# A fused RWKV5 attention and squared-ReLU FFN: a fixed issue order, W1 cast on chip, and PSUM banks allocated in pairs

## The chip, the cores and the metric

The kernel runs on one core of one Trainium2 chip. The metric is the device time of one execution in microseconds (us). Times of one kernel mostly agree within 1 to 1.5%. Every kernel below was timed against the kernel before, on the same chip, in alternating rounds. The rounds of different experiments ran at other times and on other chips, so two experiments are best compared by their ratios to the kernel before. Each profile is one execution; its span is about 2 us shorter than the device time. On a single core a run is called slow when it lies over 1.5% above the fastest run of the same kernel; comparisons use fast runs.

Engine names in the profile: PE is TensorE (matmul), PEld its weight load, DVE is VectorE, ACT is ScalarE, POOL is GpSimd, SP is SyncE, which here issues most DMAs. A `q` after the name is the engine's sequencer or its DMA queue. The granted clock (`PEclk`) is the share of its full clock that the throttle granted to TensorE. The matmuls of these kernels write to tiles in PSUM, which the code uses as eight banks of 128x512 fp32.

## The reference

```
B, H, S, D = 4, 8, 768, 48
for t in range(S):                                   # linear attention with decay
    cur = einsum('bhd,bhe->bhde', u * k[t], v[t])
    y[t] = einsum('bhd,bhde->bhe', r[t], state + cur)
    state = w * state + einsum('bhd,bhe->bhde', k[t], v[t])
x = y as rows of 384                                 # 3072 tokens x 384
h = maximum(x @ w_in, 0)                             # 384 -> 2048
out = (h * h) @ w_out                                # 2048 -> 384
```

Inputs and outputs are fp32. The kernel cuts the 3072 tokens into 24 units of 128 tokens (one batch element, one chunk of 128 steps each). The state is passed from chunk to chunk, so units 0 to 3 are the first chunk of the four batch elements, 4 to 7 the second, and so on.

## The kernel before

Each unit goes through these steps. The short names are those of the code.

- Loads of r, k and v (192 KB each, in rows of 192 bytes, since one head has 48 fp32 values).
- `kh`, `rh`: k and r times powers of the decay w. `P0`, `P1`, `du`, `dv`: the diagonal term with u. `vb`: v as bf16.
- `T`, `rkT`: transposes on PE and their copy by ACT (later units use a transposing DMA).
- `A` (8 matmuls with 48 rows, into two PSUM banks), `Bm` (DVE masks A), `Y`, `xs`, and `U`, `ts`, `S` for the state.
- `X`, `xT`: x transposed for the FFN.
- FFN for a group of two units: `F1` (x times a slice of W1, 6 matmuls of 128x256 into one PSUM bank), `re` (ReLU on ACT), `sq` (square, on ACT or on DVE; DVE multiplies the bank by the ReLU), `F2` (4 matmuls of 128x384 for a quarter of W2), then `os` and `out`.

All weights, 2 x 1.5 MB as bf16, stay in SBUF. They come by the software DMA queue of POOL, which converts fp32 to bf16 on the way. The steps are given to a small list scheduler in Python that orders them by priorities and estimated durations, and also chooses the buffer of each tile.

```python
POOLS = dict(..., bank=3, bankH=3, bankO=2, Bm=3, xs=3, xT=2, hr=6, hq=28, ...)
...
    banks = [psum.tile([128, 512], FP32, name=f"bank_{j}") for j in range(8)]
    first = {"bank": 0, "bankH": POOLS["bank"], "bankO": POOLS["bank"] + POOLS["bankH"]}

    def bank(var, pool):
        return banks[first[pool] + slot[var]]
...
    s_wb = st("wb", "SP", 0.1, dma=0.6, prio=-200, emit=lambda: nc.sync.dma_start(out=wb..., in_=flat_rows(w)))
...
            Ws.append(st(f"W{part}{s}", "POOL", 0.78, [s_g], ...))     # W1, W2: nc.gpsimd.dma_start, after a gate
...
    def f_Bm(i, e):
        def go():
            nc.vector.tensor_mul(Bmb[slot[f"Bm{i}"]][:, e], heads(f"bA{i}{e}", "bank", 128), mask_b)
...
    def f_relu(g, s):
        def go():
            hp = bank(f"bH{g},{s}", "bankH").rearrange("p (a b) -> p a b", a=2)
            nc.scalar.activation(hrb[slot[f"hr{g},{s}"]], hp, AF.Relu)
...
    def f_sq(g, s, eng):
        def go():
            hr, hq = hrb[slot[f"hr{g},{s}"]], hqb[slot[f"hq{g},{s}"]]
            if eng == "ACT":
                nc.scalar.activation(hq, hr, AF.Square)
            else:
                hp = bank(f"bH{g},{s}", "bankH").rearrange("p (a b) -> p a b", a=2)
                nc.vector.tensor_mul(hq, hp, hr)
```

No step names a semaphore. The framework sees which tiles an instruction reads and writes, and puts in the waits itself.

## Time and profile before

| | before |
|---|---|
| time, median of 3 runs (range) | 184.03 us (182.91 to 185.37) |
| span of the profile | 180.6 us |
| PE busy | 160.6 us, 89% |
| granted TensorE clock | 1.00 |
| PE busy from 60 to 160 us | 99.55 of 100 us |
| PE busy from 0 to 60 us | 44.00 of 60 us |

The profile's page of the kernel before. The first lines give each engine's busy time and its number of instructions. The next give busy tenths of each engine in 40 equal slices of the span. After that come the shares of the chain of work that ended last, and two groups of instructions with busy time, mean duration in ns, and the idle time just before them.

```profile
span 180.6 us, 4082 instructions
...
PE 160.6 (89%) x1592; PEld 118.2 (65%) x1592; DVE 128.6 (71%) x216; ACT 117.5 (65%) x214; POOL 106.8 (59%) x116
...
PE   0344769899999999999999999999999999999991
...
DVE  3399998997388838959979696778777889631310
...
DMA  3999999999949649979799799897896255221102
...
PE 79%; DVE 9%; DMA 4%; ACT 2%; SPq 2%; issue 1%; DVEq 0%
...
L604 PE MATMUL bank<-xT,W 128*128 128x256 bf16 x576 | 73.8, 273 | 0.4 <-DVE hq L629 0.3
L638 PE MATMUL bank<-W,hq 128*128 128x384 bf16 x384 | 72.0, 326 | 0.0
```

There are two regimes. After the ramp PE is busy nine tenths or more in every slice up to the end, and the FFN matmuls (L604 is F1, L638 is F2) have almost no idle time before them. In the ramp both DVE and the DMA engines are busy. The table of stretches of the kernel before says the same with numbers (start and end, length, busy us and number of instructions of each engine, granted clock, share of the DMA engines, GB/s):

```profile
core 0: us, PE busy (x) PEld busy (x) DVE busy (x) ACT busy (x) POOL busy (x), PEclk, DMA share, GB/s
10.00:15.00 5.00, 2.49 (x23) 1.60 (x23) 4.97 (x9) 1.93 (x4) 1.89 (x3) 1.00 1.06 198
...
30.00:40.00 10.00, 8.93 (x97) 7.22 (x96) 9.49 (x19) 9.82 (x19) 2.13 (x3) 1.00 1.27 185
60.00:160.00 100.00, 99.55 (x1027) 73.59 (x1026) 77.85 (x126) 69.02 (x129) 76.31 (x75) 1.00 0.78 160
```

From 10 to 15 us DVE is busy 4.97 of 5 us, and the DMA engines are full too while they move only 198 GB/s.

A piece of the chain of work of the kernel before, from its middle (start, us, what):

```profile
130.13 1.97 PE bank L604 x18
132.10 0.33 PE bank L454 x8
132.43 0.76 PE bank L604 x6
133.19 0.65 PE bank L638 x4
```

Six F1 matmuls take 0.66 us, four F2 matmuls 0.65. `A` (L454) takes 0.33 us, and the six matmuls after it 0.76, so 0.1 us more. PE does not leave the chain in this piece. The timeline of the same place (start, us, engine, line, operation, count, idle time before it and what ended it) shows why:

```profile
129.97 2.13 PE L604 MATMUL bank<-xT,W 128*128 128x256 bf16 x18
...
130.82 1.25 ACT L618 ACTIVATE hr<-bank 128x512 bf16<-128x512 f32 x2 [2.02 <-PE bank L604]
...
131.45 0.69 DVE L629 TENSOR_TENSOR hq<-bank,hr 128x512 bf16<-128x512 f32 x1 [0.28 <-ACT hr L618]
```

The 18 matmuls are three slices of F1, in three banks. ACT begins the ReLU of the first slice at 130.82 while PE goes on with the next until 132.10; DVE squares from 131.45 in the same time.

### The profile page before, as it was taken

To read this page: it belongs to the slowest core of one execution; us is meant where nothing else is said; L and a number is where in the kernel's file an instruction comes from. 1 tells how busy PE (TensorE), PEld (TensorE's weight loads), DVE (VectorE), ACT (ScalarE), POOL (GpSimd) and SP (SyncE) were. 2 spreads that over 40 slices of the span, in tenths; PEclk is the share of its full clock that TensorE was granted. 3 is DMA by queue.
4 is the path that set the end of the run, shared out by engine and by line. 5 is a ranking of instruction groups with operands and counts; after the bars stand their busy time and mean duration, and the time that the engine had idled before them with its cause. 6 is when DMAs were issued, how large, how long until landed. Compare 5 with 4: busy or idle time off the path is not lost.

```text
span 180.6 us, 4082 instructions
## 1 busy us (share of the span) xinstructions
PE 160.6 (89%) x1592; PEld 118.2 (65%) x1592; DVE 128.6 (71%) x216; ACT 117.5 (65%) x214; POOL 106.8 (59%) x116
## 2 busy tenths in 40 slices
PE   0344769899999999999999999999999999999991
PEld 0222557778766867758678677677686776777760
DVE  3399998997388838959979696778777889631310
ACT  2641528986793886827776758579298495496851
POOL 2346998024940999599879977986968980000000
PEclk9999999999999999999999999999999999999999
DMA  3999999999949649979799799897896255221102
GB/s 85 207 195 216 196 191 193 184 185 222 225 116 241 149 82 253 184 152 241 142 216 204 122 237 202 138 225 164 167 228 155 71 120 80 65 65 47 41 2 87
DMA packets 105794, 28.44 MB, mean 157 GB/s; under 512 B 98864, under 2 KB 105776, under 8 KB 105776
## 3 DMA queue, kind: packets, MB, share of 16 engines
q1 hardware_dynamic: 102064, 25.04, 68.1%
q0 software_dynamic: 3712, 3.15, 11.0%
q8 instruction: 12, 0.20, 0.5%
q14 instruction: 6, 0.05, 0.1%
HBM read 20.84 MB, written 4.72 MB: 142 GB/s over the span
## 4 chain that ended last, share of the span: by engine, by line
PE 79%; DVE 9%; DMA 4%; ACT 2%; SPq 2%; issue 1%; DVEq 0%
PE bank L638 34%; PE bank L604 32%; PE bank L454 4%; PE bank L483 3%; DMA ub<-in_u_dram 2%; DMA xT<-xs 2%; PE bank L478 2%; PE bank L429 2%; DVE rk L382 2%; SPq L351 2%; DVE xs L506 2%; DVE dv L411 2%; PE bank L495 2%; DVE Bm L467 1%; ACT rkT L436 1%
## 5 line engine op out<-in xcount | busy, mean ns | idle before, releaser
L618 ACT ACTIVATE hr<-bank 128x512 bf16<-128x512 f32 x96 | 55.9, 595 | 29.4 <-PE bank L604 27.6
L604 PE MATMUL bank<-xT,W 128*128 128x256 bf16 x576 | 73.8, 273 | 0.4 <-DVE hq L629 0.3
L638 PE MATMUL bank<-W,hq 128*128 128x384 bf16 x384 | 72.0, 326 | 0.0
L604 PEld LDWEIGHTS <-W 128*128 128x128 bf16 x576 | 55.0, 98 | 11.8 <-issue 0.9
L638 PEld LDWEIGHTS <-hq 128*128 128x128 bf16 x384 | 36.1, 98 | 19.3
L629 DVE TENSOR_TENSOR hq<-bank,hr 128x512 bf16<-128x512 f32 x48 | 32.6, 683 | 17.4 <-ACT hr L618 17.4
L467 DVE TENSOR_TENSOR Bm<-bank,maskJT 128x512 bf16<-128x512 f32 x48 | 31.1, 681 | 8.2 <-PE bank L454 8.1
L388 POOL TENSOR_TENSOR P<-ldr,ldk 128x384 f32<-128x384 f32 x24 | 28.2, 1177 | 9.9 <-DMA ldr<-in_r_dram 9.9
L528 POOL TENSOR_TENSOR S0W<-ts,WLm 128x384 bf16<-128x384 f32 x16 | 16.5, 1031 | 29.1 <-DVE ts L522 28.9
L626 ACT ACTIVATE hq<-hr 128x512 bf16<-128x512 bf16 x48 | 30.2, 630 | 1.1
L397 POOL TENSOR_TENSOR P<-P,ub 128x384 f32<-128x384 f32 x22 | 22.9, 1043 | 1.4
L411 DVE TENSOR_TENSOR dv<-ldv,du 128x384 f32<-128x384 f32 x24 | 21.2, 883 | 0.5
L506 DVE TENSOR_TENSOR xs<-bank,dv 128x384 bf16<-128x384 f32 x24 | 13.3, 555 | 11.1 <-PE bank L483 10.7
L651 ACT COPY os<-bank 128x384 f32<-128x384 f32 x24 | 11.4, 476 | 12.4 <-PE bank L638 12.1
L429 PE MATMUL bank<-identity,rk 128*128 128x128 bf16 x64 | 7.5, 273 | 10.5 <-DVE rk L382 10.2
L382 POOL TENSOR_TENSOR rk<-ldr,Wt 128x384 bf16<-128x384 f32 x16 | 16.6, 1040 | 0.1
L382 POOL TENSOR_TENSOR rk<-ldk,Wkhat 128x384 bf16<-128x384 f32 x16 | 16.0, 1002 | 0.0
L429 PEld LDWEIGHTS <-rk 128*128 128x128 bf16 x64 | 5.5, 120 | 12.4 <-DVE rk L382 11.5
L417 ACT CAST vb<-ldv 128x384 bf16<-128x384 f32 x24 | 11.6, 507 | 2.9 <-DMA ldv<-in_v_dram 2.9
L403 DVE TENSOR_REDUCE du<-P 128x8 f32<-128x384 f32 x24 | 13.0, 543 | 0.2 <-POOL P L397 0.2
L454 PE MATMUL bank<-rkT 48*128 48x128 bf16 x192 | 10.6, 233 | 2.5 <-ACT rkT L436 2.2
L483 PE MATMUL bank<-vb,Bm 128*128 128x48 bf16 x192 | 12.2, 189 | 0.4 <-DVE Bm L467 0.4
(40 smaller groups left out, 101.7 us busy)
## 6 DMA issues: line engine op xcount, KB each, us to landing
out_dram<-os SPq DMA_DIRECT2D x24, 192.0 KB, 2.6
ldk<-in_k_dram SPq DMA_DIRECT2D x11, 384.0 KB, 4.1
ldr<-in_r_dram SPq DMA_DIRECT2D x11, 384.0 KB, 5.0
ldv<-in_v_dram SPq DMA_DIRECT2D x11, 384.0 KB, 4.0
W<-in_moe_w_in_dram POOLq DMA_DIRECT2D x4, 384.0 KB, 8.9
W<-in_moe_w_out_dram POOLq DMA_DIRECT2D x4, 384.0 KB, 15.6
ldk<-in_k_dram SPq DMA_DIRECT2D x2, 192.0 KB, 4.2
ldr<-in_r_dram SPq DMA_DIRECT2D x2, 192.0 KB, 4.5
```

What stands on the lines that cost most here:

```text
L382: e.tensor_mul(rk[slot[f"rk{i}"]][:, j, :, 0:D], ld[x][slot[f"{x}P{i // 2}"]][:, i % 2], tab)
L388: nc.gpsimd.tensor_mul(P0b[slot[f"P0{i}"]], ld["r"][slot[f"rP{i // 2}"]][:, i % 2], ld["k"][slot[f"kP{i // 2}"]][:, i % 2])
L397: (nc.vector if eng == "DVE" else nc.gpsimd).tensor_mul(t, t, ub)
L411: nc.vector.tensor_mul(dvb[slot[f"dv{i}"]], ld["v"][slot[f"vP{i // 2}"]][:, i % 2], du_b)
L454: nc.tensor.matmul(heads(f"bA{i}{e}", "bank", 128)[:, hc, :], rkT[p0 : p0 + D, HP + hc, :], rkT[p0 : p0 + D, hc, :], start=True, stop=True ...
L467: nc.vector.tensor_mul(Bmb[slot[f"Bm{i}"]][:, e], heads(f"bA{i}{e}", "bank", 128), mask_b)
L483: nc.tensor.matmul(Y[:, hc, D * e : D * (e + 1)], Bm[:, e, hc, :], vb[:, 2 * hc + e, :], start=(c == 0), stop=True, skip_group_check=True,)
L604: nc.tensor.matmul(hp[:, fi, :], W1[s // 2][:, c, 128 * f : 128 * (f + 1)], xt[:, c, :], start=(c == 0), stop=(c == CCH - 1), skip_group_c ...
L618: nc.scalar.activation(hrb[slot[f"hr{g},{s}"]], hp, AF.Relu)
L626: nc.scalar.activation(hq, hr, AF.Square)
L629: nc.vector.tensor_mul(hq, hp, hr)
L638: nc.tensor.matmul(o, hqb[slot[f"hq{g},{f // 2}"]][:, f % 2, L * j : L * (j + 1)], W2[q][:, f % 4, :], start=(f == 0), stop=(f == FCH - 1) ...
```

## The change

The intent: begin the FFN earlier and shorten the ramp.

- The scheduler is removed. One long string fixes the order of all steps and the buffer of each tile.
- w and u are no longer broadcast by DMA. Four rows are loaded, and a DVE shuffle spreads them over the partitions.
- W1 comes as fp32 over the SP queue between the first loads, and ACT, DVE and POOL cast it. W2 stays on the software queue.
- The first two FFN groups have one unit (128 tokens) each.
- `A` of two units is issued back to back from unit 8 on.
- `Bm` is one DVE operation of 128x1024. For that, two banks must be one tile.
- Loads are single units, with five buffers each for r, k and v.

The diff, cut to its core (the order string alone has some 80 lines):

```diff
-def order_steps(steps, pools, sw_rate=0.75, hw_rate=0.17):
-    ...
-POOLS = dict(ldr=2, ldk=2, ldv=2, ..., bank=3, bankH=3, bankO=2, ..., xT=2, ...)
+GROUPS = [1, 1, 2, 2, 2, 2, 2, 2, 2, 2, 2, 2, 2]
+POOLS = dict(ldr=5, ldk=5, ldv=5, ws=4, ..., bank=4, bankH=2, bankO=2, ..., xT1=2, xT2=2, ...)
+ORDER = """
+w:A ld.k.3:S/0 u:S tab:A ld.k.1:S/1 ld.k.0:S/2 ld.r.0:S/0 ld.r.1:S/1 shw:D wc:S logw:A shu:D ld.r.2:S/2 Wk:A
+ld.k.2:S/3 Wt:A kh.3:G/0 ld.v.0:S/0 lW.0.2:S/0 ld.v.1:S/1 kh.1:D/1 kh.0:D/2 lW.0.0:S/1 rh.0:D lW.0.1:S/2 ...
+... T.1:P/2 dv.0:G Tc.1:D/1 Y.0:P/3 U.0:P/0 ld.r.11:S/4 cW.0.2:A S0.0:D rh.2:G xs.0:D/0
+ld.k.9:S/4 ...
-    banks = [psum.tile([128, 512], FP32, name=f"bank_{j}") for j in range(8)]
-    def bank(var, pool):
-        return banks[first[pool] + slot[var]]
+    pairs = [psum.tile([128, 2, 512], FP32, name=f"banks_{j}") for j in range(4)]
+    def bank(var, kind="b"):
+        j = first[kind] + slot[var]
+        return pairs[j // 2][:, j % 2]
-            nc.vector.tensor_mul(Bmb[slot[f"Bm{i}"]][:, e], heads(f"bA{i}{e}", "bank", 128), mask_b)
+        def Bm(e, i):
+            a = pairs[slot[f"bA{i}"] // 2].rearrange("p a (b c) -> p (a b) c", c=128)
+            e.tensor_mul(Bmb[slot[f"Bm{i}"]], a, mask_b)
+        def shw(e):
+            e.stream_shuffle(wb.rearrange("p a b -> p (a b)"), wrow, [0] * 32)
+        def AA(e, i):
+            Do.A(e, i)
+            Do.A(e, i + 1)
+        def cW(e, a, s):
+            copy(e, W1[s]..., wsb[...])          # fp32 staged in SBUF -> bf16
```

## The prediction

> **What bounds it now.** The table of stretches shows two regimes. From 40 us to the last matmul (177.1 us) TensorE is busy throughout at clock 1.00; the waits of PE list almost nothing there, and PE has 79% of the chain of waits. Six 128x256 FFN matmuls take 0.655 us, four 128x384 ones 0.65, so the FFN needs 96 x 0.655 + 96 x 0.65 = 125 us. With attention (A 0.33 + 0.1 after it, Y about 0.37, U 0.17, some transposes) I sum 153 us of PE work. The other 24 us are lost in the ramp: PE is busy 10.2 of the first 25 us, and the first FFN matmul starts at 27.5 us, when the first W1 slice lands (issued from 18.2 us). DVE is busy 4.6 to 5.0 of every 5 us between 10 and 25 us: the ramp is bound by DVE and loads (DMA share over 1.0).
>
> **What the change does.**
> 1. Broadcast loads of w and u (192 KB each, 3.6 and 4.1 us from issue to landing; u held DVE up 1.7 us) become four rows and two DVE shuffles (estimate 0.5 us each, as 384-wide DVE operations take 0.55). The queue is freed of some 2 us; the tables come 0.5 us earlier.
> 2. W1 comes over the hardware queue as fp32, between the first loads, cast by ACT, DVE and POOL. From 2 us per 384 KB load of 192 B packets I estimate 2 to 2.5 us per 786 KB slice of 2 KB packets, 1.6 us per cast; first slice at 14 us, first FFN matmul at 16. W2 stays on the software queue, its first slice earlier.
> 3. FFN groups of one unit let the FFN begin after unit 0. Their 96 matmuls are 128 wide; the transposes show 56 ns for that: 0.2 us of PE more.
> 4. In the ramp DVE work goes to POOL; Bm becomes one 128x1024 operation (two took 1.28 us; little saved).
> 5. A of two units back to back saves about 0.1 us of mode change for each of 8 pairs: 0.8 us.
> 6. FFN banks fall from 3 to 2. A bank is held 0.65 + 0.2 + 0.6 + 0.7 = 2.2 us when DVE squares, against 3.1 us between uses: little slack, so I allow 1 us of stalls.
>
> **On the critical path.** Before, PE runs without gaps from about 34.6 us, with 4.6 us of FFN done and units 0 to 3 nearly through. After, I expect this at 31 us (DVE work up to unit 3 sums to 25 us), with 8 us of FFN done. Gain 3.6 + 3.4 = 7 us, plus 0.8 for A, minus 1; the tail is unchanged.
>
> **Prediction: 176.5 us, range 171.5 to 181.5.** Faster by over 2%: 0.83; within 2%: 0.13; slower: 0.04.
>
> **What shows it.** First FFN matmul at 15 to 18 us; first F2 before 25; PE full from 29 to 32 us; waits of PE between 40 and 160 us below 2 us; one slow matmul after a pair of A, not two; PE busy sum about the same.
>
> **What would make it wrong.** Fixed order without slack: one late load (two for units 9 and 11 sit early in the queue, and W2 shares the DMA engines) stalls PE in order. Two FFN banks, or POOL and DVE holding each other up (dv took 883 ns on average instead of 555; the Trainium skill, "SBUF — State Buffer", "Who interferes with whom", describes an exclusively locked port pair), would show as PE waits in mid-kernel. If the ramp works better than I think, the gain is 10 us.

## The result, and the profile after

| | before | after |
|---|---|---|
| time, median (range) in these rounds | 184.70 us (182.91 to 185.76) | 216.94 us (214.73 to 221.09) |
| span of the profile | 180.6 us | 215.7 us |
| PE busy | 160.6 us | 167.1 us |
| PE busy, 60 to 160 us | 99.55 us | 86.46 us |
| PE busy, 0 to 60 us | 44.00 us | 37.58 us |

The ratio is 1.174, with a 95% interval of 1.165 to 1.184: slower by 17%. A ratio is the mean time of one kernel's fast runs over that of the other's fast runs of the same rounds, so it is not quite the ratio of the medians that are quoted. One of the four runs after counted as slow and is left out of the ratio. The outputs are correct.

The page of the kernel after (same parts as before):

```profile
span 215.7 us, 4244 instructions
...
PE 167.1 (78%) x1640; PEld 121.7 (56%) x1640; DVE 122.3 (57%) x196; ACT 115.5 (54%) x205; POOL 115.8 (54%) x129
...
PE   0267488479978888988988889896978788787882
...
DMA  3999999998849977788967788683252240311002
...
PE 50%; ACT 18%; DVE 16%; DMA 8%; issue 3%; SPq 3%; POOL 1%; DVEq 0%; POOLq 0%
```

PE is no longer full after the ramp: it stands at seven to nine tenths to the end. Its share of the chain fell from 79% to 50%, and ACT and DVE stepped in with 34%, though both are busy for a smaller share of the span than before. An engine that is in the chain and idle nearly half of its time is waiting in turn with the others. The table of stretches of the kernel after confirms that the loss goes on all along:

```profile
60.00:160.00 100.00, 86.46 (x881) 63.35 (x881) 66.57 (x101) 58.44 (x108) 70.70 (x71) 1.00 0.73 148
```

The granted clock is 1.00 in this stretch, so the throttle is not the cause. The chain of the kernel after at a place with no special work (start, us, what; L432 is F1, L440 the ReLU, L449 the square on DVE):

```profile
173.26 1.48 PE banks L432 x12
174.74 0.02 issue
174.76 1.09 ACT hr L440 x2
175.86 0.02 issue
175.88 0.70 DVE hq L449
176.58 0.04 issue
176.63 1.48 PE banks L432 x12
```

This is a round: two slices of F1, then two ReLUs, then a square, then F1 again. It takes 176.63 - 173.26 = 3.37 us. The timeline of the kernel after has the same moments by engine:

```profile
173.26 1.47 PE L432 MATMUL banks<-xT,W 128*128 128x256 bf16 x12
...
174.56 1.46 PE L459 MATMUL banks<-W,hq 128*128 128x384 bf16 x8
174.76 1.08 ACT L440 ACTIVATE hr<-banks 128x512 bf16<-128x512 f32 x2 [0.53 <-PE banks L432]
...
175.88 0.69 DVE L449 TENSOR_TENSOR hq<-banks,hr 128x512 bf16<-128x512 f32 x1 [3.25 <-ACT hr L440]
...
176.63 1.47 PE L432 MATMUL banks<-xT,W 128*128 128x256 bf16 x12 [0.60 <-DVE hq L449]
```

The 12 matmuls end at 174.73, and only then does the first ReLU begin, though its slice was complete after six. The square begins only when both ReLUs are done. F1 begins again only when the square is done. PE is not idle all this time: eight F2 matmuls (from 174.56) fall into the wait, and PE stands still for the last 0.60 us. But the round cannot be shorter than its chain. Before, the ReLU of one slice ran beside the matmuls of the next. The two banks of F1 now behave like one.

The waits, that is idle time of an engine by what ended it (us in total, times, longest). PE, after:

```profile
PE banks L432 <- ACT hr L440: 12.4, 16, 2.4
PE banks L432 <- DVE hq L449: 10.6, 16, 1.0
```

And ACT, after:

```profile
ACT hr L440 <- DVE hq L449: 15.7, 14, 1.7
```

A ReLU does not read the result of any square; it reads a bank that F1 filled. So I looked at the waits in the built program (the traces do not show them one by one). For the last FFN group, slices 4 to 6, where slice 4 lies in the second half of the F1 pair and slices 5 and 6 take the first half in turn, it has:

```
relu  slice 4 (second half)   waits for PE matmul 1596, the last of slice 5, into the first half
square slice 4 (second half)  waits for ACT 198, the relu of slice 5 (first half)
F1 slice 6 (first half)       waits for DVE 193, the square of slice 4 (second half)
```

Each wait is for an access to the other bank of the pair. None is needed for the result. The theory is then: **the framework guards a tile as one object. A PSUM tile of two banks has one order of accesses, and an engine that touches one half waits for other engines' last accesses to either half.**

Two rivals had to be excluded. The prediction itself offers both: **two F1 banks instead of three are too few**, and **the fixed order, or POOL and DVE holding each other up, stalls the engines**. The waits above would look much the same on the page under the first rival, since a PE that waits for a bank also waits for ReLU and square.

### The profile page after: what moved, and what is told of

It reads as the page before. It is cut to its first block, busy times and chain, and to the rows that moved or that the text cites. A ratio compares the mean times of both kernels' runs of the same rounds, so it can differ in the third digit from the quotient of the medians.

```text
span 215.7 us, 4244 instructions
## 1 busy us (share of the span) xinstructions
PE 167.1 (78%) x1640; PEld 121.7 (56%) x1640; DVE 122.3 (57%) x196; ACT 115.5 (54%) x205; POOL 115.8 (54%) x129
## 4 chain that ended last, share of the span: by engine, by line
PE 50%; ACT 18%; DVE 16%; DMA 8%; issue 3%; SPq 3%; POOL 1%; DVEq 0%; POOLq 0%
PE banks L432 32%; ACT hr L440 15%; PE banks L459 14%; DVE hq L449 11%; DMA ldv<-in_v_dram 4%; DMA ws<-in_moe_w_in_dram 3%; SPq L294 2%; DVE hr L442 1%; DMA ldk<-in_k_dram 1%; PE banks L358 1%; ACT os L248 1%; PE banks L381 1%; ACT vb L248 1%; PE banks L345 1%; ACT W L248 1%
## 5 line engine op out<-in xcount | busy, mean ns | idle before, releaser
L432 PE MATMUL banks<-xT,W 128*128 128x256 bf16 (+1 forms) x624 | 77.0, 272 | 25.5 <-ACT hr L440 12.4
L440 ACT ACTIVATE hr<-banks 128x512 bf16<-128x512 f32 x89 | 51.0, 595 | 65.4 <-PE banks L432 47.2
L432 PEld LDWEIGHTS <-W 128*128 128x128 bf16 x624 | 58.8, 101 | 43.0 <-issue 31.8
L459 PE MATMUL banks<-W,hq 128*128 128x384 bf16 x384 | 73.3, 326 | 3.9 <-DMA W<-in_moe_w_out_dram 2.6
L449 DVE TENSOR_TENSOR hq<-banks,hr 128x512 bf16<-128x512 f32 x38 | 26.3, 691 | 58.4 <-ACT hr L440 37.4
L371 DVE TENSOR_TENSOR Bm<-banks,maskJT 128x1024 bf16<-128x1024 f32 x24 | 29.0, 1216 | 2.6 <-PE banks L358 2.6
L248 ACT COPY os<-banks 128x384 f32<-128x384 f32 x22 | 10.4, 475 | 11.4 <-PE banks L459 10.3
L398 DVE TENSOR_TENSOR xs<-banks,dv 128x384 bf16<-128x384 f32 x24 | 13.1, 549 | 2.5 <-PE banks L381 1.7
L381 PE MATMUL banks<-vb,Bm 128*128 128x48 bf16 x192 | 11.6, 187 | 2.9 <-ACT vb L248 2.9
L345 PE MATMUL banks<-identity,rk 128*128 128x128 bf16 x64 | 7.3, 277 | 8.5 <-DVE rk L318 7.7
L381 PEld LDWEIGHTS <-Bm 128*128 128x128 bf16 x192 | 10.1, 99 | 5.8 <-DVE hr L442 1.8
```

Of the source, the lines that this page charges most:

```text
L248: e.copy(o, a)
L371: e.tensor_mul(Bmb[slot[f"Bm{i}"]], a, mask_b)
L381: e.matmul(y[:, hc, D * h : D * (h + 1)], m[:, HP * h + hc, :], vb[:, 2 * hc + h, :], start=(c == 0), stop=True, skip_group_check=True,)
L432: e.matmul(hp[:, fi, :], W1[f // 4][:, c, 128 * (f % 4) : 128 * (f % 4 + 1)], xt[:, c, :], start=(c == 0), stop=(c == CCH - 1), skip_group ...
L440: e.activation(hr, hp, AF.Relu)
L449: e.tensor_mul(hq, bank(f"bH{g},{s}", "bH"), hr)
```

## The experiments

All ratios are to the kernel before in the same rounds; intervals are 95%. Line numbers differ between kernels. Names with e start from the kernel after, names with b from the kernel before.

### e1: the FFN banks as tiles of their own

```diff
-    pairs = [psum.tile([128, 2, 512], FP32, name=f"banks_{j}") for j in range(4)]
+    pairs = [psum.tile([128, 2, 512], FP32, name=f"banks_{j}") for j in range(2)]
+    singles = [psum.tile([128, 512], FP32, name=f"bank_{j}") for j in range(4, 8)]
-        return pairs[j // 2][:, j % 2]
+        return pairs[j // 2][:, j % 2] if j < 4 else singles[j - 4]
```

The order of the steps, the banks and the data are those of the kernel after. Only the F1 and output banks are declared one by one.

> The changed kernel with the four FFN banks (two for the first product, two for the second) as four PSUM tiles of their own instead of two tiles of two banks; order and bank numbers untouched; the attention banks stay in two-bank tiles. Theory 1 (a two-bank tile is one object to the dependency tracking, so a matmul into one bank waits for the readers of the other): the alternation matmul, relu, square, matmul leaves the chain of waits and the time falls from 217 to 178-190 us. Theory 2 (two FFN banks are too few for a fixed order): no change, within 3% of 217. Theory 3 (late loads and a starved start): no change of the middle, at least 205.

Measured: 187.53 us, ratio 1.022 (1.016 to 1.028), correct. In the built program the ReLU of slice 4 now waits for PE matmul 1590, the last of its own slice; the square waits for its own ReLU; F1 of slice 6 waits for the ReLU of slice 5, which frees its own bank. What follows: two lines of declaration are worth 216.94 - 187.53 = 29.4 us. Since the order of the steps, the number of F1 banks and the work of every engine stay as they were, this one run speaks against both rivals. The Trainium skill, "PSUM — Partial Sum Buffer", "PSUM bank collisions raise a hardware error", says: "Semaphore-guard PSUM by **bank × quadrant** (by bank is the simple version), not by address." By that rule the waits between two banks are not needed: without them the output is correct and the simulator's check for races found none.

### e2: all eight banks as tiles of their own

```diff
-    pairs = [psum.tile([128, 2, 512], FP32, name=f"banks_{j}") for j in range(4)]
+    banks = [psum.tile([128, 512], FP32, name=f"bank_{j}") for j in range(8)]
-        return pairs[j // 2][:, j % 2]
+        return banks[first[kind] + slot[var]]
-            e.tensor_mul(Bmb[slot[f"Bm{i}"]], a, mask_b)
+            for h in range(2):
+                a = heads(banks[slot[f"bA{i}"] // 2 * 2 + h], 128)
+                e.tensor_mul(Bmb[slot[f"Bm{i}"]][:, HP * h : HP * (h + 1)], a, mask_b)
```

> All eight banks as own tiles; the mask product Bm is two 512-wide operations again, all else as in the changed kernel. Theory 1: 173-182 us, which is what the prediction expected of the whole change; the difference to the run with only the FFN banks split tells what the paired attention banks cost, expected 1 to 8 us. Theories 2 and 3: at least 205.

Measured: 186.72 us, ratio 1.017 (1.010 to 1.024), correct. This differs little from e1, so the pairs of the attention cost nothing that these rounds can show. The time lies outside the 173 to 182 us expected. From here on e2 stands for "the change without pairs". Its PE is busy 98.56 of the 100 us from 60 to 160, at the level of before (99.55), and F1's waits for ReLU and square are gone from that stretch.

The books nearly balance. From e2 to after the span grew by 215.7 - 185.1 = 30.6 us. PE idle time in the whole span went from 185.1 - 160.4 = 24.7 to 215.7 - 167.1 = 48.6, so 23.9 us more. The two PE waits above sum to 23.0 us in after and to 2.7 in e2, so they make 20.3 of it. The other 6.7 us are more busy time. One F1 matmul lasts 272 ns on average in both, one F2 matmul 326 in after and 328 in e2, so the matmuls overlap less: twelve of them take 1.48 us in the chain of after, where 18 in a row took 1.97 before.

The difference of the times, 216.94 - 186.72 = 30.2 us, is taken over different rounds, in which the kernel before took 184.70 and 183.15 us. By the ratios, 1.174 and 1.017, it is about 29 us.

What is left is e2's own loss: it is 1.7% slower than before, where 4% faster had been predicted. It arises in the ramp: in the first 60 us PE is busy 40.06 us in e2 and 44.00 before.

### b1: the kernel before, with nothing but the pairs

```diff
-    banks = [psum.tile([128, 512], FP32, name=f"bank_{j}") for j in range(8)]
+    pairs = [psum.tile([128, 2, 512], FP32, name=f"banks_{j}") for j in range(4)]
+    banks = [pairs[j // 2][:, j % 2] for j in range(8)]
```

The built program has the instructions of the kernel before in the same order on each engine. Only waits differ.

> The kernel before with one edit: its eight banks are halves of four two-bank tiles. Same instructions, order and bank numbers. Theory 1: slower by 15 to 40 us (200 to 225), with waits of PE for relu and square in the middle. Theories 2 and 3: same as before, within 1%.

Measured: 210.34 us, ratio 1.149 (1.144 to 1.153), correct. The waits of PE in b1:

```profile
PE banks L605 <- ACT hr L619: 7.3, 13, 1.3
...
PE banks L605 <- DVE hq L630: 3.3, 6, 0.9
```

The same waits appear in a kernel with three F1 banks, with the old order and without any of the new steps. The fixed order is not needed for the loss. These two waits are only part of b1's 27 us, though: all eight banks are paired here, one pair joins an attention bank with an F1 bank, and PE also waits longer for attention steps (4.2 and 2.3 us for `Bm`, for example).

### b2: the kernel before, with two F1 banks in place of three

```diff
-POOLS = dict(..., bank=3, bankH=3, bankO=2, ...)
+POOLS = dict(..., bank=4, bankH=2, bankO=2, ...)
```

> The kernel before with two FFN banks for the first product and four for attention (before: three and three), each bank its own tile; its own scheduler orders the steps for that. Theory 1: 183 to 190 us, within 3% of before. Theory 2: 200 or more.

Measured: 182.35 us, ratio 0.996 (0.992 to 1.000), correct. The table of stretches of b2:

```profile
60.00:160.00 100.00, 99.92 (x1036) 74.36 (x1034) 76.05 (x126) 71.30 (x129) 75.37 (x73) 1.00 0.78 160
```

Two banks are enough when they are two tiles. PE is full. The first rival is excluded, and nothing contradicts my arithmetic of how long a bank is held (2.2 us against 3.1 us) as long as the banks are independent. The kernel's scheduler ordered the steps anew for b2; e2 shows the same for the fixed order.

### e9: e2 with the two F1 banks, and only these, as one pair

```diff
-    banks = [psum.tile([128, 512], FP32, name=f"bank_{j}") for j in range(8)]
+    banks = [psum.tile([128, 512], FP32, name=f"bank_{j}") for j in range(4)]
+    banksH = psum.tile([128, 2, 512], FP32, name="banks_H")
+    banks += [banksH[:, j] for j in range(2)]
+    banks += [psum.tile([128, 512], FP32, name=f"bank_{j}") for j in range(6, 8)]
```

> The changed kernel with all banks as own tiles (186.7 us), save that the two banks of the first FFN product are one two-bank tile again; the second product and attention keep own tiles. If the alternation matmul, relu, square, matmul that the chain of waits shows is the loss, this pair alone brings most of the 30 us back: 205 to 217 us. If the pairs of the second product or of attention carry it, 190 us or less.

Measured: 212.75 us, ratio 1.168 (1.159 to 1.176), correct. The waits of PE in e9:

```profile
PE banks_H L435 <- ACT hr L443: 11.8, 17, 1.1
PE banks_H L435 <- DVE hq L452: 10.6, 17, 1.0
```

The F1 pair alone costs 212.75 - 186.72 = 26.0 us of the 30.2 us between e2 and after. The remaining 4 us are not clear of noise: the ratios of e9 and after, 1.168 and 1.174, have intervals that overlap (1.159 to 1.176 and 1.165 to 1.184). Whether the other pairs cost anything beside this one is therefore not shown.

### e3: e2 with the loads in the order of use

Two loads, r of unit 11 and k of unit 9, sit in the queue before those of units 4 and 5. The prediction had named them as a risk.

```diff
-... U.0:P/0 ld.r.11:S/4 cW.0.2:A ... ld.k.9:S/4 ... ld.k.5:S/2 ... ld.v.4:S/4 ... ld.r.5:S/0 ... ld.k.4:S/1
+... U.0:P/0 ld.k.5:S/1 cW.0.2:A ... ld.r.5:S/0 ... ld.k.4:S/2 ... ld.v.4:S/0 ... ld.v.5:S/4 ... ld.r.4:S/1
```

> The changed kernel with all banks as own tiles (186.7 us, 1.017 of before), and the k, r and v loads from unit 4 on issued in the order in which the units use them (in the changed kernel the loads of units 9 and 11 stand before those of 4, 6 and 7); the three early steps on units 9 and 11 that would wait for them are moved to where the other steps of these units stand. If late loads hold the fixed order up between 35 and 51 us, where PE was busy 10.5 of 15 us, r of unit 4 lands some 2 us earlier than 43.5 us and the time falls by 2 to 5 us, to 182-185. If the loss is in the two FFN banks or in DVE and POOL, it stays within 1% of 186.7.

Measured: 184.59 us, ratio 1.007 (1.002 to 1.011), correct: about 2 us better than e2, with intervals that just overlap. r of unit 4 lands at 40.4 us in its trace, 3.1 us earlier than in e2.

The trace of e2 shows what these loads hold up. A piece of its chain:

```profile
33.95 9.52 DMA ldr<-in_r_dram
```

and its table of stretches:

```profile
15.00:20.00 5.00, 3.88 (x48) 3.33 (x45) 2.98 (x7) 3.27 (x3) 3.29 (x6) 1.00 1.10 352
...
35.00:40.00 5.00, 3.52 (x43) 2.63 (x41) 2.71 (x6) 2.17 (x5) 0.89 (x1) 1.00 1.17 170
40.00:45.00 5.00, 1.93 (x17) 1.56 (x17) 1.50 (x3) 2.85 (x6) 1.31 (x2) 0.86 1.06 191
45.00:50.00 5.00, 5.00 (x50) 3.75 (x49) 3.95 (x8) 2.42 (x4) 4.31 (x5) 0.80 1.01 197
50.00:60.00 10.00, 10.00 (x100) 7.61 (x99) 7.53 (x14) 7.92 (x15) 9.27 (x10) 1.00 1.00 208
```

PE works without a gap from 29.4 to 38.5 us, much as predicted, but then it stands still for 4.6 of the next 5.6 us, and runs without a gap again from 44.1 us. From 35 to 50 us DVE is idle for nearly half of the time, and the DMA engines are full. r of unit 4 lands at 43.5 us and ends the second wait (1.8 us). The first (2.7 us) is for a ReLU, and the timeline shows why that was late: ACT stood for 2.95 us before a `vb` whose v had not landed, and the ReLU comes after it in the fixed order. So late loads and the fixed order act together here.

There is a further loss that I had not looked for: the granted clock is 0.86 from 40 to 45 us and 0.80 from 45 to 50, after these waits; the kernel before has 1.00 there. Six F1 matmuls take 1.28 us at 44.72, where 0.66 is usual, and the attention step behind them 0.96 instead of 0.54. That makes an estimate of 1 us for the clock in this stretch. It does not decide between the kernels: e5, below, has 1.00 throughout its ramp and nearly the same time.

An estimate of that landing from durations in the traces: up to r of unit 4 the queue holds 20 unit loads of 196,608 bytes (1.0 us each at the 198 GB/s seen from 10 to 15 us before), four W1 slices of 786 KB (2.25 us each at about 350 GB/s, as from 15 to 20 us above), and beside them four W2 slices on the software queue (its share of 5.6% of the span of 185.1 us, over four, is 2.6 us each). That makes 20 + 9 + 10.4 = 39.4 us of full DMA engines, plus about 3 us at the start in which the DMA engines are mostly idle (share 0.31 in the first 5 us): 42.4 us against 43.5 measured.

### e4: e3 with the second half of W2 later

```diff
-GATES = [..., [('v', 1), ('v', 1), ('v', 3), ('v', 3)]]
+GATES = [..., [('v', 1), ('v', 1), ('v', 5), ('v', 5)]]
 # and gate.1.2 W.1.2 gate.1.3 W.1.3 are moved behind the steps of unit 5 on POOL
```

> As the run with the loads in unit order, and the last two W2 slices wait for v of unit 5 instead of unit 3, so that they come after the loads of units 4 and 5 and not in front of them. If the start is bound by the loads as a whole, moving the weights behind only exchanges one wait for another: within 1% of the run with loads in order. If it is the order alone that hurts, another 2 to 4 us less, near 180.

Measured: 183.63 us, ratio 0.998 (0.992 to 1.003), correct. The waits of PE in e4:

```profile
PE bank L454 <- DMA W<-in_moe_w_out_dram: 6.1, 3, 2.7
```

Units 4 and 5 come earlier, and now F2 stands still for W2 (2.9 us in one wait in e3). Sending one load later makes another one late. The gain of 1 us over e3 is within the intervals of the two.

### e5: e2 with W1 on the software queue again

The four loads over SP and the four casts are removed; POOL issues W1 by DMA with conversion, first of all after v of unit 0.

```diff
-... lW.0.2:S/0 ... lW.0.0:S/1 ... lW.0.1:S/2 ... lW.0.3:S/3 ... cW.0.2:A ... cW.0.0:A ... cW.0.1:D ... cW.0.3:G
+... gate.0.2:G W.0.2:G W.0.0:G W.0.1:G rh.2:G W.0.3:G ...
```

> The changed kernel with all banks as own tiles, but W1 comes over the software queue as bf16, as in the kernel before, gated on v of unit 0; the fp32 copies and the four casts are gone. If the fp32 way over the hardware queue brought the first FFN matmul forward, this one starts it 2 to 4 us later (21 to 23 us against 18.3) and the time is 0 to 2 us longer; if the bytes that all loads share set the end of the ramp, the time is within 1% of 186.7.

Measured: 186.19 us, ratio 1.014 (1.009 to 1.020), correct. The first FFN matmul comes at 20.07 us, against 18.33 in e2, and a stretch of its table reads:

```profile
25.00:30.00 5.00, 0.00 (x0) 0.10 (x1) 0.56 (x1) 0.73 (x2) 4.92 (x8) 1.00 1.25 186
```

PE does nothing at all for 5 us, since the first F2 waits 6.2 us for W2, and yet the time is that of e2. I read this as: when the sum of the loads is through matters more than over which queue W1 comes. It is not shown by this run alone, and e3 has shown that order is worth about 2 us. The Trainium skill, "DMA: Bandwidth & Descriptors", "Issuing engines are not separate DMA queues", says that DMAs started by different engines end up on the same 16 DMA engines and interleave there. This agrees: 186.19 us with W1 on one queue, 186.72 us with it on the other.

### b4: the kernel before, with A in pairs and w and u as rows

Built on b2. It takes two parts of the change that looked good by themselves: `A` of units i and i + 1 as one step from unit 8 on, and the DVE shuffle in place of the broadcast loads.

```diff
+            A = st(f"AA{i}", "PE", 0.66, [rkT[i], rkT[i + 1]], ..., alloc=[four banks],
+                   emit=lambda i=i: (f_A(i)(), f_A(i + 1)()))
-    s_wb = st("wb", "SP", 0.1, dma=0.6, ..., emit=lambda: nc.sync.dma_start(out=wb..., in_=flat_rows(w)))
+    s_wr = st("wrow", "SP", 0.1, dma=0.05, ..., emit=lambda: nc.sync.dma_start(out=quarter_rows(wrow), in_=row4(w)))
+    s_wb = st("wb", "DVE", 0.55, [s_wr], ..., emit=lambda: nc.vector.stream_shuffle(wb..., wrow, [0] * 32))
```

> The kernel before with its own scheduler, two FFN banks and four attention banks as own tiles (182.35 us, 0.996 of before), A of two units back to back from unit 8 on, and w and u as four rows and a shuffle. From the traces a pair of A costs 0.66 us with its transition against 2 x 0.44, so 8 pairs give 1.8 us, and the rows 0.5 to 1 us: 179 to 181.5 us, 0.98 to 0.99 of before.

Measured: 182.30 us, ratio 0.994 (0.990 to 0.998), correct. I had expected more. PE's busy sum did fall, from 161.4 us in b2 to 159.3, but PE now waits elsewhere:

```profile
PE bank L625 <- ACT hr L639: 2.8, 5, 0.7
```

A step that needs two units at once and four banks together may leave the scheduler less to fill gaps with; that is an argument and was not tested. What the traces show is that from 40 to 160 us PE is busy 117.56 us, against 119.92 in b2. Most of the saved matmul time came back as waits. b4 is still the fastest correct kernel in ratio, by 0.6% over before (interval 0.2 to 1.0%). It is 0.2% ahead of b2, which the intervals do not separate.

### e6: e4 with the first F2 later on PE

Since e4's PE stands in order behind F2 that waits for W2, the twelve first F2 steps and their outputs were moved behind the attention of units 4 and 5.

```diff
-... F2.1.2:P ... F2.0.2:P ... F2.1.3:P ... F2.0.3:P ... F2.3.0:P/1 ... F2.2.0:P/0 ... F2.2.1:P ... F2.2.2:P ... T.7:P/0
+... T.7:P/0 ... F2.1.2:P F2.0.2:P F2.1.3:P os.1:A/0 F2.0.3:P out.1:S os.0:A/1 F2.3.0:P/1 out.0:S F2.2.0:P/0 F2.2.1:P F2.2.2:P
```

> The run with the loads in order and the last two W2 slices behind them (183.6 us, 0.998 of before), in which PE stood still for 1.3 and 2.2 us between 40.9 and 45.9 us because the second halves of F2 of units 0 and 1 stand in the fixed order before attention work of unit 4 and FFN work of groups 2 and 3 that was ready; here they, and what follows from them, stand behind that work. If the fixed order turned late loads into idle time, 2 to 4 us go: 179.5 to 181.5 us, 0.975 to 0.987 of before. If it is only the sum of the loads, the wait returns later and the time stays within 0.5%.

Measured: 184.15 us, ratio 1.004 (1.001 to 1.008), correct. No gain. The table of stretches of e6:

```profile
40.00:45.00 5.00, 1.87 (x30) 1.25 (x29) 4.57 (x7) 1.31 (x3) 5.00 (x7) 1.00 1.26 191
```

PE waited 2.7 us for one `Bm` of DVE in place of waiting for W2. The idle time stayed; only its name changed. In this stretch POOL is busy all 5 us and DVE 4.57, and the chain runs over POOL from 35.8 to 41.0 us and over DVE from there to 44.2. So with the loads of W2 moved back, it is POOL and DVE in their fixed order that PE waits for here, and no longer a load. It stays open what an order that is searched anew for these loads would give.

### e7 and e8: less weight to load

If the sum of loads binds the ramp, then a kernel with fewer bytes must be faster, by about the DMA time that is taken away. e7 loads half of W2 and uses it twice; e8 loads half of W1 as well. Both give wrong outputs and exist only for their times.

```diff
+    W2[2:] = W2[:2]                       # e7 and e8; the loads W.1.2 and W.1.3 are removed
+    W1[1], W1[3] = W1[0], W1[2]           # e8; loads and casts of slices 1 and 3 are removed
```

> Wrong result on purpose. The changed kernel with all banks as own tiles (186.7 us), its order as it was, but the third and fourth W2 slices are not loaded: F2 reads the first and second in their place, same matmuls. If the loads set the end of the ramp, r of unit 4 lands some 5 us earlier than 43.5 us and the time falls by 3 to 5 us, to 181.5-184. If DVE work sets it (which the prediction held), no change within 1%.

> Wrong result on purpose. As the run with half of W2, and the second and fourth W1 slices are not loaded nor cast either (the first and third serve twice): about 10 us of DMA time less in the ramp in all. If the loads set the end of the ramp, PE is full from about 40 us instead of 51 and the time is 177 to 180 us, about what the prediction gave. If DVE work sets it, less than 2 us go (DVE loses one cast of 0.95 us, POOL one of 1.5).

Measured: e7 180.01 us, ratio 0.984 (0.980 to 0.987); e8 176.93 us, ratio 0.966 (0.962 to 0.972). The kernel before had nearly the same median in the rounds of e7 and e8 (183.28 us) as in those of e2 (183.15 us), so the times may be compared. By the durations above, e7 saves 2 x 2.6 = 5.2 us of DMA and gains 6.7 us on e2; e8 saves 5.2 + 2 x 2.25 = 9.7 us and gains 9.8 us. The table of stretches of e8:

```profile
40.00:45.00 5.00, 5.00 (x52) 3.51 (x49) 4.57 (x10) 2.38 (x6) 4.56 (x6) 1.00 0.79 170
```

PE is full from 40 to 45 us here, where in e2 it is busy 1.93 of 5 us. The step that uses r of unit 4 begins at 43.5 us in e2, at 38.3 in e7 and at 35.5 in e8. So this step comes 5.2 and 8.0 us earlier, and the time falls by about the DMA time taken away. Three reservations: e8 also drops two of the four casts, so its gain is not of the loads alone. e7 drops no cast, but gains more than its DMA time, and its 180.01 us lie below the 181.5 to 184 expected. And only part of the gain is idle time of PE, which falls by 3.5 us in e7 and 6.2 in e8; its busy time falls by 2.2 and 3.7 us.

## Why the prediction was wrong, point by point

**The main error: step 6 of the prediction.** It reads "FFN banks fall from 3 to 2. A bank is held 0.65 + 0.2 + 0.6 + 0.7 = 2.2 us when DVE squares, against 3.1 us between uses: little slack, so I allow 1 us of stalls." The sum takes the two banks as independent. They are the two halves of one tile, and the framework orders all accesses to a tile, so that F1, ReLU and square of both banks follow one another. Where 1 us of stalls was allowed, that cost 30.2 us (216.94 to 186.72, e2). The F1 pair alone makes 26.0 of them (e9), and the pairs alone put 27 us on the kernel before (b1). That two banks as such cost nothing is shown by b2. The line `pairs = ...` was in the diff; I used it only to cost `Bm`. It could have been costed as a round in series: two ReLUs of 0.55 us, a square of 0.7 and twelve matmuls of 1.3 to 1.5 us make 3.1 to 3.3 us for two slices, and the chain shows 3.37. The FFN has 96 slices' worth, so an estimate is 48 x 3.37 = 162 us for the FFN, with F2 in the waits, even before any attention work falls into its path, against the 125 us of the prediction.

The Trainium skill, "Perfetto Trace Analysis", "Matmuls", says that independent matmul groups should rotate through different PSUM banks, so that ACT and DVE empty one while the next is filled. The kernel after does rotate through two banks and gains nothing from it; e1, with the same banks as two tiles, does.

**The second error: the length of the ramp.** The prediction says "After, I expect this at 31 us (DVE work up to unit 3 sums to 25 us)", and took it that PE would have no gaps from there on. DVE was relieved as planned: from 10 to 40 us it is busy 19.0 of 30 us in e2, against 28.45 before. PE did start to run without gaps at 29.4 us, but only until 38.5: then the loads of units 4 and 5 bind. r of unit 4 lands at 43.5 us, PE runs without gaps from 44.1 us, and at full clock only from 50 us. Bringing W1 and W2 forward puts an estimated 19 us of DMA time (4 x 2.25 + 4 x 2.6) in front of units 4 and 5. What is left of the error without the pairs is 186.72 - 176.5 = 10.2 us. e7 and e8 show that it falls with the load time. That e8's 176.93 us is nearly the time predicted proves nothing by itself, since e8 loads less than the kernel predicted. e3 shows that about 2 us of it are order, namely the two early loads that the prediction named as a risk. The lower clock after the waits (an estimate of 1 us) and the A pairs that did not pay (0.8 us predicted, b4) belong to it too; how the 10.2 us divide exactly is not shown.

**What was right, or nearly.** The first FFN matmul comes at 19.07 us (18.33 in e2) instead of 27.48; I had said 15 to 18. The first F2 comes at 25.03 us, where "before 25" was said. The shuffles took 0.58 us each, and a cast 1.47 us on ACT, and the tables came 0.24 us earlier (Wkhat at 4.80 us instead of 5.04) rather than 0.5. A in pairs works: in the chain of the kernel after,

```profile
151.07 0.55 PE banks L358 x16
151.62 0.76 PE banks L459 x4
```

a pair of A takes 0.55 us and lengthens the F2 group behind it from 0.65 to 0.76, so it costs 0.66 us. Before, two single ones cost 2 x (0.33 + 0.10) = 0.86 us. A pair saves 0.2 us, twice what I had said, but b4 shows that the gain turns into waits.

**What was wrong in the signs to look for.** "Waits of PE between 40 and 160 us below 2 us": from 60 to 160 us alone PE idles 13.5 us. "PE busy sum about the same": 167.1 instead of 160.6 us in after, though 160.4 in e2.

**What the prediction feared.** It named "two FFN banks, or POOL and DVE holding each other up". Waits of PE in mid-kernel came as described, so the symptom was right and both causes were wrong: b2 excludes the number of banks, e1 removes the waits with the order and the work of POOL and DVE unchanged, and `dv`, the operation that had shown the slow mean, takes 868 ns on DVE after against 883 before, hence no worse.

**What stays open.** Whether an order exists that keeps the early FFN and does not delay units 4 and 5; e4 and e6 each moved the wait without removing it. What the pairs other than F1's cost beside it is not clear of noise. No correct kernel tried here beats the kernel before by more than 0.6%.

## What to carry to other kernels

Where a framework puts in the waits, a tile is the unit of waiting: declare each PSUM bank that is to be double-buffered as a tile of its own, and when a change merges tiles for one wide operation, ask who else uses them. In a trace the sign is a matmul, an activation and a vector operation that follow each other in the chain with all three engines partly idle, and an engine that waits for an operation whose result it does not read. In a ramp, add up the DMA time that stands in the queues before the load that releases the next stage; here, moving work off a busy engine gained nothing, and the order of the loads about 2 us, while that sum stayed as it was.

## What the Trainium skill lacked or had wrong

- "PSUM — Partial Sum Buffer" gives the rule by bank, but neither it nor another page that I read says that a PSUM tile of several banks, declared as one, is guarded as one object by the framework. Here this cost 26.0 us for one pair (212.75 against 186.72 us, e9) and 27 us in an otherwise unchanged kernel (b1).
- "DMA: Bandwidth & Descriptors", "Specifications", names 512 bytes as the least transfer for full rate, but neither that section nor another that I read has a measured rate on trn2 for full queues of such short rows. Here the loads in rows of 192 bytes moved 198 GB/s with the DMA engines full (before, 10 to 15 us), and 352 GB/s went through while the W1 slices in rows of 2 KB came (e2, 15 to 20 us).
